# Retention and expert routing on one core: token keys of both heads in one place, scaled in place, and the state beside the values

## The chip, the cores and the metric

The kernel runs on 1 core of one Trainium2 chip. The metric is the device time of one execution in microseconds (us), lower is better. A core has TensorE (PE, with its weight loads shown apart as PEld), VectorE (DVE), ScalarE (ACT), GpSimd (POOL) and SyncE (SP), which here only issues DMAs and reads registers. The input loads and the weight loads are issued by SP, the token stores by ACT, and indirect gathers and scatters by POOL.

## What is computed

The reference has two halves. The first is retention, an attention with a decay in place of a softmax (8 batches, 8 heads, 576 positions, heads of 64):

```python
scores = scale * np.matmul(q, k.transpose(0, 1, 3, 2))
gamma = 1.0 - 2.0 ** (-5.0 - np.arange(H, dtype=np.float32))
Dmat = np.where(rel >= 0, gamma[:, None, None] ** rel[None, :, :], 0.0)   # rel = i - j
ret = scores * Dmat[None, :, :, :]
return np.matmul(ret, v).astype(np.float32)
```

Its output, laid out as 4608 tokens of 512 features, goes through the second half: tokens whose product with w_skip is not positive pass unchanged; each other token goes to the one of 8 experts with the greatest logit, which adds gate * (relu(x @ w1) @ w2), with 1024 hidden features, to it.

## The kernel before

**The retention stage.** The 4608 tokens are worked on in 36 groups of 128 tokens (NT = 36). A group is two chunks (c = 0, 1) of 64 positions, and nine chunks (NQ = 9) are one batch element. Heads go in four pairs (NPR = 4), one head of a pair on partitions 0 to 63, the other on 64 to 127; j counts the two. Retention is computed by chunks: the products inside a chunk (scores, line 469), and a running state of 64 by 64 for each head that carries what earlier chunks gave (state, line 520). For a group g the loop at line 697 does:

- keys(g + 1) on POOL (line 508): the keys by token, scaled by a table of decays, are written to a tile kn of two buffers. There are two operations of 64 partitions, since the keys of the two j lie in different places of the loaded tile.
- state(2g) and scores(2g + 2), in turn on PE: products of kn with the values are summed up in the PSUM tile ps_s, products of queries and keys go to psc. After each state comes a pair of ACT copies (line 542) of ps_s into the tile u of the next chunk, where the next products of values need it. The next state product adds to the same ps_s and so waits for the copies.
- values(2g - 2) and values(2g - 1) on PE (line 552): one product with 128 rows each takes 64 rows of values and 64 rows of state as its weights, and decayed scores and queries as the moving side. So the state must lie in the same place of u as the values, on the other half of the partitions.
- state(2g + 1) and scores(2g + 3), then decay(g + 1) on DVE (line 489), which multiplies scores by decays and writes them over u's keys by feature.
- stage_c (line 580): transposes on PE, an ACT copy, and the store of a finished group of tokens by ACT. In between come logits (every four groups), pieces of routing on PE and DVE (a list with due times, line 657), and, once the first expert is known, its weights (line 634): SP loads them, ACT and POOL split them into a high and a low part.

**The tile u and its loads.** u_g holds four places (s) of [2 chunks, 4 pairs, 64] float32, 2 KB in each partition. Partitions 0 to 63 hold in s = 0 to 3 queries, keys, values by token, keys by token; partitions 64 to 127 hold keys, queries, keys by token, values by token. It is loaded by two DMAs of 512 KB (load_half, line 433): places 0 and 1, the first half, and places 2 and 3, the second. There are five buffers (UBUFS) and loads are issued four groups ahead (UAHEAD). At the start of iteration g the first half of group g + 4 is asked for (line 700); its buffer is that of group g - 1, which is free after values(2g - 1). After the first block of products the second half of group g + 3 is asked for, with a dependence on that block (line 705). Both are on SP's queue, in which everything goes in order: a waiting DMA holds what is behind it, and so does the register load that reads the first expert's number (line 321).

The state copy for j writes u[halves[j], 3 - j], which holds the raw keys by token of that half. So it may only be written when keys has read them. At the start of a batch element the state is zero, and a memset on POOL (line 525) writes zeros there instead.

**Order.** PE's order is that of the program (manual_schedule, line 667). On the other engines a scheduler orders instructions by their dependences, except those put under keep_in_program_order.

**After the retention stage.** Expert 0's rows are gathered by POOL, whose index comes from DVE (close_first, line 282), and turned by early transposes (line 615). The experts then run from about 170 us to the end: products on PE in three float32r terms, weights loaded by SP, split by ACT and DVE.

Of the kernel before, what the change touches and what calls it, by code (L numbers as in the profile page):

```python
# [11 lines left out]
F32 = mybir.dt.float32  # L12
# [5 lines left out]
ALU = mybir.AluOpType  # L18
# [3 lines left out]
B, H, S, D = 8, 8, 576, 64  # L22
NTOK, DM, NE, DF = B * S, H * D, 8, 1024
P = 128
NT = NTOK // P
NQ = S // D
NPR = H // 2
# [15 lines left out]
UAHEAD = 4  # L43
UBUFS = UAHEAD + 1
# [12 lines left out]
def kernel(  # L57
# [9 lines left out]
    nc = tc.nc  # L67
# [15 lines left out]
    def keep_up(n):  # L83
        for _ in range(n):
            nc.tensor.matmul(ps_m, warm[:, :P], warm, start=True, stop=True)
# [329 lines left out]
    with ExitStack() as actx:  # L415
        ac = actx.enter_context(tc.tile_pool(name="ac", bufs=1))
        ap = actx.enter_context(tc.tile_pool(name="ap", bufs=2))
# [5 lines left out]
        tt_sb = ac.tile([P, 3, NQ + 1, NPR], F32, tag="tt", name="tt_sb")  # L423
# [5 lines left out]


        u_t = {}

        def load_half(g, s, after=None):
            if s == 0:
                u_t[g] = ap.tile([P, 4, 2, NPR, D], F32, tag="u", name=f"u_{g}", bufs=UBUFS)
            half = nc.sync.dma_start(
                u_t[g][:, s : s + 2].rearrange("p s c a i -> p (s c a i)"),
                qkv[g, s // 2],
            )
            if after is not None:  # L440
                tc.add_manual_dep(
                    half.ins,
                    after.name,
                    mybir.DependencyInfo(mybir.DependencyClass.Sync, mybir.DependencyReason.DATA),
                    reason="the second half begins behind a block of products",
                )

        def load_u(g):
            for s in (0, 2):
                load_half(g, s)  # L450

        def last_product():
            return next(i for i in reversed(nc.cur_bb.bb.instructions) if i.engine == mybir.EngineType.PE)
# [7 lines left out]
        nc.scalar.dma_start(wg_sb, wg)  # L461

        ps_s = pp.tile([P, NPR, D], F32, tag="s", name="ps_s")
        halves = [slice(0, D), slice(D, P)]
        kn_t, px_t = {}, {}

        psc_t = {}

# [38 lines left out]

        def keys(g):
            c0 = 2 * g % NQ
            kn_t[g] = ap.tile([P, 2, NPR, D], F32, tag="kn", name=f"kn_{g}")  # L510
            for j in range(2):
                h = halves[1 - j]
                nc.gpsimd.tensor_tensor(  # L513
                    kn_t[g][h],
                    u_t[g][h, 2 + j],
                    tt_sb[h, 0, c0 : c0 + 2, :].unsqueeze(3).broadcast_to([D, 2, NPR, D]),
                    ALU.mult,
                )

        def state(n):  # L520

            g, c = divmod(n, 2)
            if n % NQ == 0:
                for j in range(2):
                    nc.gpsimd.memset(u_t[g][halves[j], 3 - j, c], 0.0)
            if n % NQ == NQ - 1:
                return
            for a in range(NPR):
                for j in range(2):
                    h = halves[1 - j]  # L530
                    nc.tensor.matmul(  # L531
                        ps_s[halves[j], a, :],
                        kn_t[g][h, c, a, :],
                        u_t[g][h, 3 - j, c, a, :],
                        start=n % NQ == 0 and a == 0,
                        stop=a == NPR - 1,
                        skip_group_check=True,
                    )
                    yield
            g, c = divmod(n + 1, 2)  # L540
            for j in range(2):
                nc.scalar.copy(u_t[g][halves[j], 3 - j, c], ps_s[halves[j]])  # L542

        def in_turn(*products):

            products = list(products)
            while products:
                products = [p for p in products if next(p, p) is not p]
# [3 lines left out]
        def values(n):  # L552

            g, c = divmod(n, 2)
            if c == 0:
                px_t[g] = pp.tile([P, NPR, P], F32, tag="xt", name=f"pxt_{g}", bufs=2)
            pxt = px_t[g]
            for a in range(NPR):
                for j in range(2):
                    nc.tensor.matmul(  # L560
                        pxt[halves[j], a, c * D : (c + 1) * D],
                        u_t[g][:, 3 - j, c, a, :],
                        u_t[g][:, j, c, a, :],
                        start=c == 0 and a == 0,
                        stop=c == 1 and a == NPR - 1,
                        skip_group_check=True,
                    )
            if c == 1:
                b, o = divmod(g, NB)
                if o == 0:  # L570
                    xt_t[b] = ap.tile([P, NPR, NB * P], F32, tag="xt", name=f"xt_{b}")
                c0 = 2 * g % NQ
                nc.vector.tensor_tensor(
                    xt_t[b][:, :, o * P : (o + 1) * P].rearrange("p a (c i) -> p a c i", c=2),
                    pxt.rearrange("p a (c i) -> p a c i", c=2),
                    gt_sb[:, c0 : c0 + 2].rearrange("p c a i -> p a c i"),
                    ALU.mult,
                )
# [89 lines left out]
        mctx.__enter__()  # L668
        lt = None
        keys(0)  # L670
        def route(b):

# [23 lines left out]

        for g in range(NT):
            ahead = g + 1 < NT
            if g + UAHEAD < NT:
                load_half(g + UAHEAD, 0)  # L700
            if ahead:
                keys(g + 1)
            in_turn(state(2 * g), *([scores(2 * g + 2)] if ahead else []))
            if UAHEAD <= g + UAHEAD - 1 < NT and g:
                load_half(g + UAHEAD - 1, 2, last_product())
            if g < len(NKEEP):
                keep_up(NKEEP[g])
            if g:
                values(2 * g - 2)
                values(2 * g - 1)  # L710
            if g < 4:
                decays(g + 1)
            in_turn(state(2 * g + 1), *([scores(2 * g + 3)] if ahead else []))
            if ahead:
                decay(g + 1)
            if g >= 2:
                stage_c(g - 2)
            if lt is None:
                routing(0 if g == NT - 1 else 3 if g < starts[KCUT + 1] else 8)
            if lt is not None:  # L720
                logits_b(g // NB - 1 - (g % NB < 2), lt)
                route(g // NB - 1 - (g % NB < 2))
                lt = None
            if g > NB and g % NB == 1:
                lt = logits_a(g // NB - 1)
            weights()
        g = NT
# [25 lines left out]
    block = rt.tile([P, 1], F32, tag="block", name="block")  # L753
# [211 lines left out]
    with tc.For_i(0, nblock, 1):  # L965
# [31 lines left out]
        for f in range(NFC):  # L997
            if f + AHEAD < NFC:
                ws.append(split_w(load_w(0, f + AHEAD, [reg])))
            h = [mp.tile([P, CAP], F32R, tag=x, name=f"{x}_more_{f}", bufs=3) for x in ("hhi", "hlo")]  # L1000
# [64 lines left out]
```

## Time and profile before

| What | Value |
|---|---|
| Median of 3 runs | 438.65 us (432.28 to 443.81) |
| The profiled execution | 432.73 us |
| Its span, first to last instruction | 431.0 us |
| Mean granted TensorE clock | 0.983 |
| Instructions | 13306 |
| DMA traffic | 92.14 MB, 214 GB/s over the span |
| Loads of u | 72 of 512 KB, median 5.2 us from issue to landing |

The profile is of one execution. Busy times add up the records of an engine; matmuls overlap in their records, so a busy PE is not one at its peak. A row of a timeline is start, duration, engine, line, operation, output and inputs, shape, count, and in brackets the idle time before it with what ended it. A row of waits is engine, line, what it waited for, and us in total, number, longest. What ended a wait is inferred: of several it is the one that came last in this profile.

### The profile page before, as it was taken

To read this page: it belongs to the slowest core of one execution; us is meant where nothing else is said; L and a number is where in the kernel's file an instruction comes from. 1 tells how busy PE (TensorE), PEld (TensorE's weight loads), DVE (VectorE), ACT (ScalarE), POOL (GpSimd) and SP (SyncE) were. 2 spreads that over 40 slices of the span, in tenths; PEclk is the share of its full clock that TensorE was granted. 3 is DMA by queue.
4 is the path that set the end of the run, shared out by engine and by line. 5 is a ranking of instruction groups with operands and counts; after the bars stand their busy time and mean duration, and the time that the engine had idled before them with its cause. 6 is when DMAs were issued, how large, how long until landed. Compare 5 with 4: busy or idle time off the path is not lost. (4 is left out here: it accounts for less than half of the span.)

```text
span 431.0 us, 13306 instructions
## 1 busy us (share of the span) xinstructions
PE 391.7 (91%) x5482; PEld 351.7 (82%) x5484; DVE 276.3 (64%) x562; ACT 186.9 (43%) x360; POOL 160.4 (37%) x182
## 2 busy tenths in 40 slices
PE   7788988899988589999999999999999999999990
PEld 3576776677777467888999999999999999999980
DVE  2595598488589978848755554865654755656430
ACT  2255444454644457117444434444444445445210
POOL 4665564545555397150330042033141250400302
PEclk9899999999999989999999999999999999999996
DMA  8899989899986977255673455455465465642101
GB/s 311 301 326 314 344 304 314 313 327 307 365 310 232 338 284 240 98 149 207 203 230 117 146 172 193 147 173 185 150 212 172 162 207 173 200 144 77 52 0 52
DMA packets 29023, 92.14 MB, mean 214 GB/s; under 512 B 4119, under 2 KB 4247, under 8 KB 28960
## 3 DMA queue, kind: packets, MB, share of 16 engines
q1 hardware_dynamic: 19584, 71.31, 48.4%
q0 software_dynamic: 3616, 9.86, 6.7%
q10 hardware_dynamic: 5760, 10.09, 6.3%
q8 instruction: 44, 0.72, 0.7%
q14 instruction: 19, 0.16, 0.1%
HBM read 77.07 MB, written 14.55 MB: 213 GB/s over the span
## 5 line engine op out<-in xcount | busy, mean ns | idle before, releaser
L140 DVE TENSOR_TENSOR wlo_w<-w,whi_w 128x1024 fp32r<-128x1024 f32 x59 | 71.9, 1223 | 61.9 <-ACT whi_w L139 61.8
L513 POOL TENSOR_TENSOR kn<-u,tt_sb 64x512 f32<-64x512 f32 x72 | 77.3, 1073 | 67.2 <-PE psc L479 44.2
L843 POOL DMA_INDIRECT out<-rs,sidx x24 | 32.8, 1366 | 156.4 <-DVE rs L842 153.2
L139 ACT CAST whi_w<-w 128x1024 fp32r<-128x1024 f32 x59 | 61.6, 1051 | 61.5 <-PE py L387 59.4
L542 ACT COPY u<-ps_s 64x256 f32<-64x256 f32 x128 | 47.0, 367 | 65.6 <-issue 26.7
L387 PE MATMUL py<-hhi,whi_w 128*128 128x344 f32 (+6 forms) x224 | 70.6, 315 | 0.0
L387 PE MATMUL ph<-xhi,whi_w 128*128 128x344 f32 (+6 forms) x224 | 68.9, 308 | 0.0
L387 PE MATMUL py<-hhi,wlo_w 128*128 128x344 f32 (+6 forms) x224 | 67.8, 303 | 0.0
L387 PE MATMUL ph<-xhi,wlo_w 128*128 128x344 f32 (+6 forms) x224 | 67.8, 302 | 0.0
L387 PE MATMUL ph<-xlo,whi_w 128*128 128x344 f32 (+6 forms) x224 | 67.7, 302 | 0.0
L387 PE MATMUL py<-hlo,whi_w 128*128 128x344 f32 (+6 forms) x224 | 67.6, 302 | 0.0
L531 PE MATMUL ps_s<-u,kn 64*64 64x64 f32 x1024 | 48.8, 227 | 14.4 <-issue 6.4
L531 PEld LDWEIGHTS ps_s<-u,kn 64*64 64x64 f32 x1024 | 39.2, 135 | 26.8 <-issue 10.8
L495 DVE TENSOR_TENSOR u<-psc,dt_sb 64x512 f32<-64x512 f32 x72 | 49.6, 689 | 14.2 <-PE psc L479 8.9
L395 ACT ACTIVATE hhi<-ph 128x344 fp32r<-128x344 f32 (+8 forms) x61 | 26.0, 427 | 64.1 <-PE ph L387 57.0
L479 PE MATMUL psc<-u 64*64 64x64 f32 x1152 | 51.8, 227 | 1.9 <-DVE u L495 0.6
L560 PE MATMUL pxt<-u 128*64 128x64 f32 x1152 | 45.1, 231 | 3.2 <-issue 2.8
L479 PEld LDWEIGHTS psc<-u 64*64 64x64 f32 x1152 | 41.7, 136 | 5.3 <-issue 2.4
L560 PEld LDWEIGHTS pxt<-u 128*64 128x64 f32 x1152 | 39.1, 142 | 7.5 <-issue 4.6
L387 PEld LDWEIGHTS py<-hhi,whi_w 128*128 128x128 f32 x224 | 42.2, 188 | 0.9
L387 PEld LDWEIGHTS ph<-xhi,whi_w 128*128 128x128 f32 x224 | 42.3, 189 | 0.1
L387 PEld LDWEIGHTS ph<-xlo,whi_w 128*128 128x128 f32 x224 | 42.3, 189 | 0.1
(178 smaller groups left out, 645.0 us busy)
## 6 DMA issues: line engine op xcount, KB each, us to landing
u<-qkv SPq DMA_DIRECT2D x72, 512.0 KB, 5.2
w<-w SPq DMA_DIRECT2D x64, 512.0 KB, 3.7
out<-xn ACTq DMA_DIRECT2D x36, 256.0 KB, 5.4
out<-rs,sidx POOLq DMA_INDIRECT x24
xg<-out,gidx POOLq DMA_INDIRECT x21
dt_sb<-dtab ACTq DMA_DIRECT2D x1, 256.0 KB
gt_sb<-dtab ACTq DMA_DIRECT2D x1, 256.0 KB
wg_sb<-wg ACTq DMA_DIRECT2D x1, 64.0 KB, 8.8
```

The source lines that it names most:

```text
L139: nc.scalar.copy(hi, t)
L140: nc.vector.tensor_tensor(lo, t, hi.bitcast(F32), ALU.subtract)
L387: nc.tensor.matmul(ps, x, y, start=first and n == 0, stop=last and n == 3 * len(terms) - 1)
L395: nc.scalar.activation(hi, ph, AF.Relu)
L479: nc.tensor.matmul(psc_t[g][halves[j], c, a, :], u[halves[j], 1 - j, c, a, :], u[halves[j], j, c, a, :], start=c == 0 and a == 0, stop=c = ...
L495: nc.vector.tensor_tensor(u_t[g][h, j], psc[halves[j]], dt_sb[h, c0 : c0 + 2], ALU.mult)
L513: nc.gpsimd.tensor_tensor(kn_t[g][h], u_t[g][h, 2 + j], tt_sb[h, 0, c0 : c0 + 2, :].unsqueeze(3).broadcast_to([D, 2, NPR, D]), ALU.mult,)
L531: nc.tensor.matmul(ps_s[halves[j], a, :], kn_t[g][h, c, a, :], u_t[g][h, 3 - j, c, a, :], start=n % NQ == 0 and a == 0, stop=a == NPR - 1, ...
L542: nc.scalar.copy(u_t[g][halves[j], 3 - j, c], ps_s[halves[j]])
L560: nc.tensor.matmul(pxt[halves[j], a, c * D : (c + 1) * D], u_t[g][:, 3 - j, c, a, :], u_t[g][:, j, c, a, :], start=c == 0 and a == 0, stop ...
L843: put = nc.gpsimd.indirect_dma_start(out=out, out_offset=bass.IndirectOffsetOnAxis(ap=sidx[:n, k, e : e + 1], axis=0), in_=rs[:n], in_offs ...
```

## The change

u gets a fifth place. The second half is now loaded by two DMAs of 64 partitions and 256 KB each: partitions 0 to 63 (values, keys) into places 2 and 3, partitions 64 to 127 (keys, values) into places 3 and 4. So the keys by token of both halves lie in place 3 (KEYS), and one POOL operation of 128 partitions scales them in place; the tile kn is gone (4 KB in each partition with its two buffers, while five u tiles grow by 10 KB). The values of partitions 0 to 63 lie in place 2, those of 64 to 127 in place 4, and the other 64 partitions of these two places are free: the state is copied, and the zeros are written, there. The products take the same operands at their new places.

The loads of u are put under program order, and the first half of group g + 4 is asked for behind the values products of iteration g, after the second half of group g + 3; in iteration 0 it stays at the start.

```diff
@@ -429,21 +429,32 @@
 
 
         u_t = {}
+        halves = [slice(0, D), slice(D, P)]
+
+        V0, KEYS, V1 = 4, 3, 2
+        vals = (V0, V1)
 
         def load_half(g, s, after=None):
             if s == 0:
-                u_t[g] = ap.tile([P, 4, 2, NPR, D], F32, tag="u", name=f"u_{g}", bufs=UBUFS)
-            half = nc.sync.dma_start(
-                u_t[g][:, s : s + 2].rearrange("p s c a i -> p (s c a i)"),
-                qkv[g, s // 2],
-            )
-            if after is not None:
-                tc.add_manual_dep(
-                    half.ins,
-                    after.name,
-                    mybir.DependencyInfo(mybir.DependencyClass.Sync, mybir.DependencyReason.DATA),
-                    reason="the second half begins behind a block of products",
+                u_t[g] = ap.tile([P, 5, 2, NPR, D], F32, tag="u", name=f"u_{g}", bufs=UBUFS)
+                places = ((slice(0, P), 0),)
+            else:
+                places = tuple((halves[j], V1 + j) for j in range(2))
+            for rows, k in places:
+                half = tc.keep_in_program_order(
+                    nc.sync.dma_start(
+                        u_t[g][rows, k : k + 2].rearrange("p s c a i -> p (s c a i)"),
+                        qkv[g, s // 2, rows],
+                    )
                 )
+                if after is not None:
+                    tc.add_manual_dep(
+                        half.ins,
+                        after.name,
+                        mybir.DependencyInfo(mybir.DependencyClass.Sync, mybir.DependencyReason.DATA),
+                        reason="the second half begins behind a block of products",
+                    )
+            return half
 
         def load_u(g):
             for s in (0, 2):
@@ -461,8 +472,7 @@
         nc.scalar.dma_start(wg_sb, wg)
 
         ps_s = pp.tile([P, NPR, D], F32, tag="s", name="ps_s")
-        halves = [slice(0, D), slice(D, P)]
-        kn_t, px_t = {}, {}
+        px_t = {}
 
         psc_t = {}
 
@@ -507,22 +517,17 @@
 
         def keys(g):
             c0 = 2 * g % NQ
-            kn_t[g] = ap.tile([P, 2, NPR, D], F32, tag="kn", name=f"kn_{g}")
-            for j in range(2):
-                h = halves[1 - j]
-                nc.gpsimd.tensor_tensor(
-                    kn_t[g][h],
-                    u_t[g][h, 2 + j],
-                    tt_sb[h, 0, c0 : c0 + 2, :].unsqueeze(3).broadcast_to([D, 2, NPR, D]),
-                    ALU.mult,
-                )
+            k = u_t[g][:, KEYS]
+            ins = nc.gpsimd.tensor_tensor(
+                k, k, tt_sb[:, 0, c0 : c0 + 2, :].unsqueeze(3).broadcast_to([P, 2, NPR, D]), ALU.mult
+            )
 
         def state(n):
 
             g, c = divmod(n, 2)
             if n % NQ == 0:
                 for j in range(2):
-                    nc.gpsimd.memset(u_t[g][halves[j], 3 - j, c], 0.0)
+                    nc.gpsimd.memset(u_t[g][halves[j], vals[j], c], 0.0)
             if n % NQ == NQ - 1:
                 return
             for a in range(NPR):
@@ -530,8 +535,8 @@
                     h = halves[1 - j]
                     nc.tensor.matmul(
                         ps_s[halves[j], a, :],
-                        kn_t[g][h, c, a, :],
-                        u_t[g][h, 3 - j, c, a, :],
+                        u_t[g][h, KEYS, c, a, :],
+                        u_t[g][h, vals[j], c, a, :],
                         start=n % NQ == 0 and a == 0,
                         stop=a == NPR - 1,
                         skip_group_check=True,
@@ -539,7 +544,7 @@
                     yield
             g, c = divmod(n + 1, 2)
             for j in range(2):
-                nc.scalar.copy(u_t[g][halves[j], 3 - j, c], ps_s[halves[j]])
+                nc.scalar.copy(u_t[g][halves[j], vals[j], c], ps_s[halves[j]])
 
         def in_turn(*products):
 
@@ -559,7 +564,7 @@
                 for j in range(2):
                     nc.tensor.matmul(
                         pxt[halves[j], a, c * D : (c + 1) * D],
-                        u_t[g][:, 3 - j, c, a, :],
+                        u_t[g][:, vals[j], c, a, :],
                         u_t[g][:, j, c, a, :],
                         start=c == 0 and a == 0,
                         stop=c == 1 and a == NPR - 1,
@@ -696,8 +701,8 @@
 
         for g in range(NT):
             ahead = g + 1 < NT
-            if g + UAHEAD < NT:
-                load_half(g + UAHEAD, 0)
+            if g == 0:
+                load_half(UAHEAD, 0)
             if ahead:
                 keys(g + 1)
             in_turn(state(2 * g), *([scores(2 * g + 2)] if ahead else []))
@@ -708,6 +713,8 @@
             if g:
                 values(2 * g - 2)
                 values(2 * g - 1)
+                if g + UAHEAD < NT:
+                    load_half(g + UAHEAD, 0)
             if g < 4:
                 decays(g + 1)
             in_turn(state(2 * g + 1), *([scores(2 * g + 3)] if ahead else []))
```

## The prediction

> **What bounds the kernel now.** I read the page first, then the busy time by stage, the timelines of ACT, POOL, DVE, PE and SP, and last the DMA queues. These are the page's lines:
>
> ```profile
> span 431.0 us, 13306 instructions
> ...
> PE 391.7 (91%) x5482; PEld 351.7 (82%) x5484; DVE 276.3 (64%) x562; ACT 186.9 (43%) x360; POOL 160.4 (37%) x182
> ...
> q1 hardware_dynamic: 19584, 71.31, 48.4%
> q0 software_dynamic: 3616, 9.86, 6.7%
> q10 hardware_dynamic: 5760, 10.09, 6.3%
> ```
>
> The edit touches only the retention stage, which ends near 166 us; the first four of the next rows are stretches of it, the fifth is of the experts' stage. Columns: length, busy time of PE, PEld, DVE, ACT and POOL, PE clock, DMA share, GB/s.
>
> ```profile
> 10.00:15.00 5.00, 2.85 (x69) 1.81 (x69) 1.95 (x3) 1.95 (x6) 4.33 (x6) 0.90 1.02 410
> ...
> 21.60:137.00 115.40, 101.36 (x2861) 82.12 (x2860) 88.62 (x176) 57.51 (x139) 64.11 (x71) 1.00 0.91 320
> ...
> 139.00:147.00 8.00, 5.65 (x185) 5.05 (x180) 7.56 (x29) 3.12 (x7) 0.28 (x2) 1.00 0.86 290
> 147.00:166.00 19.00, 14.23 (x310) 10.93 (x310) 16.22 (x33) 10.34 (x22) 18.11 (x23) 0.91 0.80 287
> ...
> 200.00:240.00 40.00, 40.00 (x250) 38.68 (x249) 23.32 (x32) 17.70 (x27) 7.32 (x6) 1.00 0.60 199
> ```
>
> In the experts' stage PE has no gap, so what the retention stage gives up reaches the end. On POOL the keys of groups 4 and 32 begin at:
>
> ```profile
> 21.60 2.49 POOL L513 TENSOR_TENSOR kn<-u,tt_sb 64x512 f32<-64x512 f32 x2 [0.59 <-POOL kn L513]
> ...
> 136.93 2.18 POOL L513 TENSOR_TENSOR kn<-u,tt_sb 64x512 f32<-64x512 f32 x2 [2.16 <-PE psc L479]
> ```
>
> That is 115.3 us for 28 groups, 4.12 us each. What sets that period is seen on ACT in a stretch without routing work:
>
> ```profile
> 104.43 0.74 ACT L542 COPY u<-ps_s 64x256 f32<-64x256 f32 x2 [1.76 <-PE psc L479]
> ...
> 106.20 0.74 ACT L542 COPY u<-ps_s 64x256 f32<-64x256 f32 x2 [0.41 <-PE psc L479]
> ...
> 107.89 0.74 ACT L542 COPY u<-ps_s 64x256 f32<-64x256 f32 x2 [0.95 <-issue]
> ```
>
> Two pairs of state copies make a group, 1.7 to 1.8 us apart: a block of products, a pair of copies that frees ps_s, the next block. That chain gives 3.46 us (107.89 less 104.43); routing and logits add the rest up to 4.12. The keys are not on it, though the trace names POOL as a releaser:
>
> ```profile
> 41.38 2.15 POOL L513 TENSOR_TENSOR kn<-u,tt_sb 64x512 f32<-64x512 f32 x2 [1.30 <-PE psc L479]
> ...
> 41.63 0.74 ACT L542 COPY u<-ps_s 64x256 f32<-64x256 f32 x2 [1.26 <-issue]
> ...
> 42.48 0.29 PE L531 MATMUL ps_s<-u,kn 64*64 64x64 f32 x2 [0.66 <-POOL kn L513]
> ```
>
> PE starts at 42.48, just behind the copies (41.63 + 0.74 = 42.37); the first half of kn happens to end at 42.45. POOL's operation at 41.38 makes the keys of the group after, so it is not what PE needs. I therefore count no gain from keys in the steady stretch.
>
> There is one place where the keys do hold PE:
>
> ```profile
> SPq L321 <- DVE lead_id L261: 7.2, 1, 7.2
> ...
> 139.87 0.81 SPq L436 DMA_DIRECT2D u<-qkv  x2
> ...
> 146.83 2.15 POOL L513 TENSOR_TENSOR kn<-u,tt_sb 64x512 f32<-64x512 f32 x2 [7.72 <-PE ps_m L188]
> ...
> 149.01 0.74 ACT L542 COPY u<-ps_s 64x256 f32<-64x256 f32 x2 [3.98 <-POOL kn L513]
> ...
> 149.86 0.24 PE L531 MATMUL ps_s<-u,kn 64*64 64x64 f32 x1 [3.16 <-ACT u L542]
> ```
>
> SP waits 7.2 us for the first expert's number, and the loads behind it (the first half of group 34, then the second of 33) go out only at 139.87. Keys 33 begin at 146.83, when, as I read it, that second half has landed (PE, the named releaser, had used the old kn long before). They end at 148.98. The state copy at 149.01 overwrites raw keys, so it must wait for both key operations, and PE stands 3.16 us.
>
> **The change part by part.** Durations are those of the profiled execution: 432.73 us in all, 431.0 of it span.
>
> *Keys.* 72 operations become 36 over 128 partitions.
>
> ```profile
> L513 POOL TENSOR_TENSOR kn<-u,tt_sb x72: 1033/1042/1422, 6.7 to 158.0; 64x512 f32<-64x512 f32 x72
> ...
> L648 POOL TENSOR_TENSOR wlo_w<-w,whi_w x20: 717/726/744, 148.9 to 169.4; 128x256 fp32r<-128x256 f32 x20
> ```
>
> The price of one lies between 1.04 us (the same 512 elements in each partition) and 2 x 0.73 = 1.45 us (128 partitions, half the elements, doubled). I take 1.04: the row with the same operands and length. POOL loses 25 to 40 us of its 77 us of keys. In the steady stretch this is worth 0 by itself, since the copy chain sets the period. If the cover went, it would cost one key operation a group.
>
> *State copies and memsets.* As many and as long as before, to free places; the wait of copies and memsets on the raw keys goes. In the steady stretch 0 (above). At 149 us the copy no longer waits; PE can then begin its block when keys 33 and the first half of 34, whose scores share the block, are there. Second half 33 is now queued ahead of first half 34, so it lands about one transfer earlier and the first half takes its old landing, about 146.8. One 512 KB transfer costs 48.4% x 431 / 71.31 = 2.93 us for each MB, 1.53 us for 0.524 MB. Keys 33: 146.83 - 1.53 + 1.04 = 146.3. PE can start near 146.9 where it started at 149.86: **-3.0 us**. Late next is the gather of expert 0's rows: its index comes from DVE, which is busy 16.2 of 19 us here, and its landing already holds PE at the stage's end:
>
> ```profile
> 157.19 0.80 DVE L295 TENSOR_SCALAR gi<-ids 128x2 int32<-128x2 f32 x1
> ...
> 166.61 0.98 PE L620 MATMUL pt_early<-ident,xg 128*128 128x128 f32 x7 [0.70 <-DMA xg<-out,gi]
> ```
>
> If the gather does not move, almost nothing of the 3.0 passes: bounds 0 and -4.3 (3.0 and the 1.3 us that the granted clock of 0.91 costs in 14.2 us of PE work). I keep -3.0, because the shorter POOL time moves DVE too, as follows.
>
> *DVE behind POOL.* Small DVE operations stretch while a key operation runs:
>
> ```profile
> 123.86 2.17 POOL L513 TENSOR_TENSOR kn<-u,tt_sb 64x512 f32<-64x512 f32 x2 [2.31 <-PE psc L479]
> ...
> 124.09 0.84 DVE L170 TENSOR_TENSOR cum<-cum,cs 128x8 f32<-128x8 f32 x1
> ...
> 125.05 1.00 DVE L204 TENSOR_TENSOR gt<-gt,cp 128x8 f32<-128x8 f32 x1
> ...
> L228 DVE TENSOR_SCALAR r<-iota,trank x36: 304/315/1906, 65.8 to 178.8; 128x384 bf16<-128x384 f16 x36
> ...
> 131.94 2.95 DVE L228 TENSOR_SCALAR r<-iota,trank 128x384 bf16<-128x384 f16 x5
> ...
> 138.43 0.15 DVE L261 CAST lead_id<-top 128x1 int32<-128x1 f32 x1
> ```
>
> Each ends as one of the two key operations ends (124.93, 126.03). Five matches that take 5 x 0.315 = 1.6 us took 2.95, on the way to the expert's number at 138.43, for which SP waits. With about half of POOL's key time gone, the number comes some 1 us earlier, and so do the loads behind it. On PE I take **-1.0 us** over the four stretches of routing; bounds 0 (DVE idle elsewhere) and -5.
>
> *Loads.* The second half becomes two DMAs of 64 partitions and 256 KB: 36 more issues.
>
> ```profile
> L436 SPq DMA_DIRECT2D u<-qkv x72: 327/328/1287, 0.8 to 145.5; - x72
> ...
> SPq L436 <- PE psc L479: 69.7, 30, 4.7
> ...
> 138.40 1.15 PE L560 MATMUL pxt<-u 128*64 128x64 f32 x32
> ```
>
> 36 x 0.33 = 11.8 us of SP, inside the 69.7 us in which SP waits for PE anyway: 0; uncovered, 0.33 us a group. Before, the first half of g+4 waited for the values products of iteration g, and the second half of g+3 stood behind it. Now the second half goes when its block of products is done, the 1.15 us of values products sooner, and the first half, not needed until iteration g+3, gives way. That is 0 on the path in steady state.
>
> What 64 partitions cost the DMA engines, no row shows. Bounds: 0, as the price by the byte does not depend on size (2.93 us per MB on q1 and on q0, 2.69 on q10's 256 KB stores), and +1.53 us a group, if a half reaches half the engines' throughput. The DMA engines are busy 0.91 x 115.4 / 28 = 3.75 us of a group's 4.12, so up to +0.37 us a group is covered. The nearest row, q0's gathers and scatters, has blocks of fewer than 128 rows among it and is no dearer than whole loads; I take +0.2, which is covered: 0. [...] No row of this trace shows a transfer to one half.
>
> *Start.* POOL waits there for each second half (keys 1 at 10.39), with DMA full at 410 GB/s:
>
> ```profile
> 10.39 2.20 POOL L513 TENSOR_TENSOR kn<-u,tt_sb 64x512 f32<-64x512 f32 x2 [1.24 <-DMA u<-qkv]
> ...
> 12.62 0.74 ACT L542 COPY u<-ps_s 64x256 f32<-64x256 f32 x2 [1.91 <-POOL kn L513]
> ```
>
> One key operation is saved (-1.1); halves at the dear bound would land 3.1 us later by group 1. I take 0.
>
> **Sum:** 432.73 - 3.0 - 1.0 = 428.7. The profiled execution lies 5.9 us below the median of the runs, 438.65 (432.28 to 443.81); the same 4 us off that median gives 434.7. I forecast the middle, 431.7, and for this case alone 427 to 436.
>
> **The rivals.**
> *Slower: the DMA engines become the bound.* If the halves cost more than +0.37 us a group, the loads fall behind and the period is the DMA time. Halfway to the dear bound, +0.77, gives 4.52 us a group: 0.40 x 32 groups loaded after the start = 12.8, so 445.5. At the bound 5.28, +37, so 470. For it: the 0.91 share, and 1.02 in the start. Against it: the price by the byte is flat in three queues. [...]
> *Nothing moves.* The gather's index comes no earlier and PE waits at the early transposes for what it gained: 432.7. For it: DVE is busy 7.56 of 8 us from 139 to 147, and PE already waits there. Against it: DVE has POOL's stretches to lose.
> *A larger gain.* DVE gets all of its -5 and the tail its -4.3: 423.4. For it: the fast groups show 3.46 us, the mean is 4.12. Against it: PE's own logits and routing products fill part of that.
> *The wait merely moves:* if keys 33 still end last, since both of their transfers land late, the stall is about 1.2 us shorter instead of 3.0, 430.5; it lies inside the forecast.
>
> **How the numbers follow.** Forecast 0.45 (the moved wait in it), DMA bound 0.27, nothing 0.16, larger gain 0.12. A measurement here tells about 2%, some 9 us. Faster by more than that: the larger gain and 0.08 of the forecast, 0.20. Slower: nearly all of the DMA case, 0.25. Within: the other 0.55. The range 423 to 452 leaves out about 0.06 below and 0.11 above, where the halves cost more than about +1.0 us a group (432.73 + 32 x 0.6 = 452).
>
> **What would show it.** Right: 36 key operations near 1.04 us; no wait of ACT's state copies on POOL near 147 us and a PE wait there under 0.5 us; steady period 4.0 to 4.1 us a group with a DMA share still under 0.97; lead_id 1 us earlier; the stage over by 163 us. Wrong: a DMA share at 1.0 with fewer than 310 GB/s, POOL's keys waiting for DMA in group after group, scores products held by loads (the slower rival); or the early transposes waiting 3 us or more for the gather (nothing moves).

## The result, and the profile after

| | before | after |
|---|---|---|
| Median, us | 437.12 (432.28 to 443.81, 4 runs) | 458.95 (452.74 to 461.42, 4 runs) |
| Profiled execution, us | 432.73 | 456.71 |
| Mean granted TensorE clock | 0.983 | 0.953 |

The changed kernel is slower: ratio 1.050, 95% interval 1.040 to 1.060. The forecast was 431.7 us, with a range of 423 to 452. Ratios here and below leave out executions more than 1.5% above the fastest of the same kernel; the profiled ones of the first three experiments are among these and some 1% longer than the rest. These are the page's lines for it, the last two those of the issues of u's loads (number, size, us to landing):

```profile
span 455.0 us, 13348 instructions
...
PE 401.2 (88%) x5482; PEld 360.0 (79%) x5484; DVE 262.0 (58%) x562; ACT 187.5 (41%) x360; POOL 120.7 (27%) x146
...
q1 hardware_dynamic: 20160, 71.31, 54.1%
q0 software_dynamic: 3616, 9.86, 6.4%
q10 hardware_dynamic: 5760, 10.09, 6.3%
...
u<-qkv SPq DMA_DIRECT2D x36, 512.0 KB, 5.3
u<-qkv SPq DMA_DIRECT2D x72, 256.0 KB, 6.2
```

The same 71.31 MB on q1 hold the DMA engines for 54.1% of 455.0 us, 246.2 us; before it was 48.4% of 431.0, 208.6 us. The difference, 37.6 us, is 1.04 us for each of the 36 groups. On that queue only the number and shape of the second halves and the order of the loads changed; experiments below take number and order by themselves. The busy time by stage, in the same columns as before the change, shows what follows:

```profile
10.00:15.00 5.00, 2.94 (x36) 1.81 (x37) 0.69 (x1) 0.73 (x2) 2.85 (x5) 0.50 1.06 277
21.60:137.00 115.40, 94.13 (x2465) 76.55 (x2461) 66.92 (x140) 48.83 (x117) 29.92 (x35) 0.93 1.00 281
27.57:157.00 129.43, 105.93 (x2778) 86.07 (x2778) 76.53 (x176) 55.38 (x133) 33.95 (x40) 0.93 1.00 284
```

In the stretch from 21.60 to 137.00 the DMA share went from 0.91 to 1.00 and the rate from 320 to 281 GB/s: the DMA engines are full and move less. PE's granted clock fell from 1.00 to 0.93 there, but PE is idle for 21 of the 115 us. POOL's busy time fell from 64.11 to 29.92 us, and that bought nothing. The waits between 20 and 160 us and the one-line view of the keys say who stands for it:

```profile
POOL u L521 <- DMA u<-qkv: 60.0, 21, 4.2
```

```profile
L521 POOL TENSOR_TENSOR u<-u,tt_sb x36: 1033/1044/1557, 10.1 to 184.2; 128x512 f32<-128x512 f32 x36
```

Before, POOL's keys waited for a load in 4 places of 72. Now they wait for one 21 times in these 140 us. POOL's timeline places the loss; its rows are the keys of groups 0, 4, 32, 33 and 35, and the first expert's weights between them:

```profile
10.12 1.56 POOL L521 TENSOR_TENSOR u<-u,tt_sb 128x512 f32<-128x512 f32 x1 [7.03 <-DMA u<-qkv]
...
27.57 1.04 POOL L521 TENSOR_TENSOR u<-u,tt_sb 128x512 f32<-128x512 f32 x1 [3.48 <-DMA u<-qkv]
...
157.02 1.04 POOL L521 TENSOR_TENSOR u<-u,tt_sb 128x512 f32<-128x512 f32 x1 [2.71 <-DMA u<-qkv]
167.79 2.78 POOL L653 TENSOR_TENSOR wlo_w<-w,whi_w 128x256 fp32r<-128x256 f32 x4 [9.73 <-DMA u<-qkv]
170.53 1.05 POOL L521 TENSOR_TENSOR u<-u,tt_sb 128x512 f32<-128x512 f32 x1
...
184.20 1.03 POOL L521 TENSOR_TENSOR u<-u,tt_sb 128x512 f32<-128x512 f32 x1
```

Their counterparts before, beside the rows of groups 4 (21.60), 32 (136.93) and 33 (146.83) in the prediction:

```profile
6.73 1.04 POOL L513 TENSOR_TENSOR kn<-u,tt_sb 64x512 f32<-64x512 f32 x1 [3.64 <-DMA u<-qkv]
...
148.94 2.79 POOL L648 TENSOR_TENSOR wlo_w<-w,whi_w 128x256 fp32r<-128x256 f32 x4
...
156.92 1.04 POOL L513 TENSOR_TENSOR kn<-u,tt_sb 64x512 f32<-64x512 f32 x1
```

The early transposes, where the retention stage ends, on PE after the change and before it:

```profile
190.14 1.09 PE L625 MATMUL pt_early<-ident,xg 128*128 128x128 f32 x8
```

```profile
165.58 0.33 PE L620 MATMUL pt_early<-ident,xg 128*128 128x128 f32 x1
```

So the loss adds up like this:

| Stretch | before | after | difference |
|---|---|---|---|
| Start, to keys 4 | 21.60 | 27.57 | +6.0 |
| Keys 4 to keys 32, 28 groups | 115.3 (4.12 each) | 129.5 (4.62 each) | +14.1 |
| Keys 32 to keys 35 | 20.0 | 27.2 | +7.2 |
| Keys 35 to the early transposes | 8.7 | 5.9 | -2.7 |
| The rest of the span | 265.4 | 264.9 | -0.6 |

The sum is the 24.0 us between the spans. The experts' stage is unchanged. All of the loss is in the stage that loads u.

### The profile page after: what moved, and what is told of

It reads as the page before. It is cut to its first block, busy times and chain, and to the rows that moved or that the text cites. A ratio compares the mean times of both kernels' runs of the same rounds, so it can differ in the third digit from the quotient of the medians.

```text
span 455.0 us, 13348 instructions
## 1 busy us (share of the span) xinstructions
PE 401.2 (88%) x5482; PEld 360.0 (79%) x5484; DVE 262.0 (58%) x562; ACT 187.5 (41%) x360; POOL 120.7 (27%) x146
## 3 DMA queue, kind: packets, MB, share of 16 engines
q1 hardware_dynamic: 20160, 71.31, 54.1%
## 5 line engine op out<-in xcount | busy, mean ns | idle before, releaser
L536 PE MATMUL ps_s<-u 64*64 64x64 f32 x1024 | 53.4, 238 | 18.0 <-POOL u L521 9.7
L536 PEld LDWEIGHTS ps_s<-u 64*64 64x64 f32 x1024 | 42.4, 145 | 32.3 <-issue 15.7
L521 POOL TENSOR_TENSOR u<-u,tt_sb 128x512 f32<-128x512 f32 x36 | 39.1, 1087 | 98.3 <-DMA u<-qkv 71.6
L489 PE MATMUL psc<-u 64*64 64x64 f32 x1152 | 57.4, 239 | 3.9 <-issue 3.9
L565 PE MATMUL pxt<-u 128*64 128x64 f32 x1152 | 46.6, 234 | 12.5 <-issue 12.5
L578 DVE TENSOR_TENSOR xt<-pxt,gt_sb 128x512 f32<-128x512 f32 x36 | 24.9, 692 | 52.0 <-PE pxt L565 48.5
L565 PEld LDWEIGHTS pxt<-u 128*64 128x64 f32 x1152 | 40.3, 145 | 16.7 <-issue 13.9
L489 PEld LDWEIGHTS psc<-u 64*64 64x64 f32 x1152 | 45.9, 147 | 6.9 <-issue 4.4
```

What stands on the lines that cost most here:

```text
L489: nc.tensor.matmul(psc_t[g][halves[j], c, a, :], u[halves[j], 1 - j, c, a, :], u[halves[j], j, c, a, :], start=c == 0 and a == 0, stop=c = ...
L521: ins = nc.gpsimd.tensor_tensor(k, k, tt_sb[:, 0, c0 : c0 + 2, :].unsqueeze(3).broadcast_to([P, 2, NPR, D]), ALU.mult)
L536: nc.tensor.matmul(ps_s[halves[j], a, :], u_t[g][h, KEYS, c, a, :], u_t[g][h, vals[j], c, a, :], start=n % NQ == 0 and a == 0, stop=a == N ...
L565: nc.tensor.matmul(pxt[halves[j], a, c * D : (c + 1) * D], u_t[g][:, vals[j], c, a, :], u_t[g][:, j, c, a, :], start=c == 0 and a == 0, st ...
L578: nc.vector.tensor_tensor(xt_t[b][:, :, o * P : (o + 1) * P].rearrange("p a (c i) -> p a c i", c=2), pxt.rearrange("p a (c i) -> p a c i", ...
```

## Experiments

The theory after the result: a transfer that reaches partitions 0 to 63 alone, or 64 to 127 alone, holds the DMA engines much longer by the byte, and the loss is this and nothing else (the half theory). The rivals: the mere number of DMAs and of their issues (count), the pinned order of the loads (order), the keys scaled in place and the fifth place (layout), and later a limit on DMAs in flight.

**One part at a time.** The kernel before, with only its second half loaded as two DMAs of 64 partitions:

```diff
+            places = (slice(0, P),) if s == 0 else (slice(0, D), slice(D, P))
+            for rows in places:
-            half = nc.sync.dma_start(u_t[g][:, s : s + 2]..., qkv[g, s // 2])
+                half = nc.sync.dma_start(u_t[g][rows, s : s + 2]..., qkv[g, s // 2, rows])
...
```

> The kernel before, in which only the second half of each group's load is split into two DMAs of 64 partitions and 256 KB; places, keys, order as before. Half theory (a transfer to the partitions 0 to 63, or 64 to 127, alone costs the DMA engines nearly twice by the byte): the whole loss, 450 to 460 us, the SP queue's share of the engines' time up by 37 us as in the changed kernel, 4.5 to 4.7 us a group. Count theory (each more DMA costs a fixed time): the same. Order theory (the loads' new order on SP is what costs) and place theory (scaling in place, the fifth place): 433 to 440 us, 4.1 us a group.

Measured: 470.42 us, ratio 1.085 (1.075 to 1.095). This one part makes all of the loss, and more. From its page, and SP's waits between 20 and 140 us:

```profile
q1 hardware_dynamic: 20160, 71.31, 50.7%
...
L515 POOL TENSOR_TENSOR kn<-u,tt_sb 64x512 f32<-64x512 f32 x72 | 76.6, 1063 | 99.7 <-DMA u<-qkv 70.0
```

```profile
SPq L438 <- PE pxt L562: 72.2, 21, 9.3
```

q1 takes 239.9 us (50.7% of 473.2). That is 31 us more than before, where the half theory expected 37, yet the time rose by more than that. From keys 4 (26.89) to keys 32 (176.43) a group takes 5.34 us, above the expected 4.5 to 4.7, at a DMA share of 0.88. That is 4.70 us of the engines' time, close to the 4.62 of the change; the rest of the period is waiting. Here the second half of group g + 3 still stands in SP's queue behind the first half of g + 4, which waits 72.2 us for the values products; before the change it was 21.5 us in the same stretch. SP also waits 12.6 us there for three stores to land. The change itself lost less (1.050), and its order of loads, which takes the second half out from behind that wait, is by this reading what saves the rest. No run separates it from the keys scaled in place.

The second half as two DMAs by places instead, each of 256 KB over all 128 partitions:

```diff
+            parts_ = ((s, 2, 0, 2 * DM),) if s == 0 else ((s, 1, 0, DM), (s + 1, 1, DM, DM))
+            for k, m, c0, n in parts_:
+                half = nc.sync.dma_start(u_t[g][:, k : k + m]..., qkv[g, s // 2, :, c0 : c0 + n])
```

> The kernel before, in which the second half of each load is split into two DMAs of 256 KB by places, each over all 128 partitions (rows of 2 KB). As many DMAs as in the change, none to one half. Half theory: 433 to 441 us, the SP queue's time up by under 8 us. Count theory: 450 to 460 us. Order and place theories: 433 to 440 us.

Measured: 440.06 us, ratio 1.015 (1.006 to 1.024). The same number of DMAs, of the same size, costs 1.5% where it reaches all partitions, and q1's time is 213.2 us (48.1% of 443.2), 4.6 more than before. By the medians the count explains less than a third of the 5%, and by its interval less than half.

The kernel before with only the new order of the loads and program order for them:

```diff
-            if g + UAHEAD < NT:
-                load_half(g + UAHEAD, 0)
+            if g == 0:
+                load_half(UAHEAD, 0)
...
                 values(2 * g - 1)
+                if g + UAHEAD < NT:
+                    load_half(g + UAHEAD, 0)
```

> The kernel before with the change's order of loads alone: under program order, the second half of group g+3 ahead of the first half of g+4, which comes behind the values products. Half and count theories: no loss, 428 to 438 us; by my prediction's step for the tail the PE wait of 3.2 us near 150 us falls under 1 us, worth up to 3 us. Order theory: 445 us or more.

Measured: 435.83 us over 10 runs, ratio 1.004 (0.999 to 1.009). POOL, PE and DVE at the place where the prediction took 3.0 us:

```profile
147.49 2.16 POOL L515 TENSOR_TENSOR kn<-u,tt_sb 64x512 f32<-64x512 f32 x2 [6.32 <-DMA u<-qkv]
```

```profile
150.53 0.24 PE L533 MATMUL ps_s<-u,kn 64*64 64x64 f32 x1 [1.78 <-POOL kn L515]
...
157.03 0.28 PE L233 MATMUL ps_m<-mc,r 128*128 128x40 bf16 x3 [1.66 <-DVE r L228]
...
170.89 0.98 PE L622 MATMUL pt_early<-ident,xg 128*128 128x128 f32 x7 [1.82 <-DMA xg<-out,gi]
```

```profile
161.97 0.17 DVE L295 TENSOR_SCALAR gi<-ids 128x2 int32<-128x2 f32 x1
```

PE's wait fell from 3.16 to 1.78 us, not under 1 as expected, and PE then waits 1.66 us for the matches on DVE, and at the stage's end 1.82 us for the gather where it waited 0.70. The index gi comes no earlier than before (157.19). The order is worth nothing.

The change with its second half loaded whole:

```diff
-                places = tuple((halves[j], V1 + j) for j in range(2))
+                places = ((slice(0, P), V1),)
+                nc.gpsimd.memset(u_t[g][halves[1], V0], 0.0)
```

> The changed kernel, but the second half is one DMA of 128 partitions to places 2 and 3, and place 4 of partitions 64 to 127 is set to zero by POOL. It leaves out the values of half the heads (their output is zero), so tokens go to other experts and only the retention stage is to be compared. Half and count theories: 4.0 to 4.15 us a group, a DMA share of 0.93 or less, the keys of group 32 before 138 us. Order and place theories: 4.5 to 4.7 us a group as in the changed kernel, a DMA share of 0.97 to 1.

Measured: 474.81 us in all. This is no verdict, since other tokens go to other experts and the experts' stage grows. The retention stage can be compared. Keys 4 begin at 18.87 and keys 32 at 132.97:

```profile
18.87:132.97 114.10, 99.52 (x2858) 81.22 (x2856) 83.53 (x174) 57.34 (x138) 48.25 (x69) 1.00 0.93 323
```

That is 4.07 us a group (114.10 / 28) where the change has 4.62 and the kernel before 4.12. Everything of the change is in this run except the halves and the 36 more DMAs that they bring. Layout falls as a cause of the loss, and the start's loss is gone too (18.87 against 27.57).

**The transfers by themselves.** The next kernel only loads: twelve second halves in one form after another, with a DVE copy behind each form that ends it.

```python
for phase in phases:
    for i in range(12):
        phase(i)
    nc.vector.tensor_copy(sink, big[:, :, 0 : 2 * DM : DM // 2])
```

> Transfers alone: it leaves out the whole computation (the output is zeros). Ten phases of 12 second halves each, one phase after the other: whole (512 KB, 128 partitions); two DMAs to partitions 0 to 63 and 64 to 127 on SP; the same with the second on ACT's queue; two DMAs of 128 partitions by columns; four DMAs of 32 partitions, the halves in turn; four DMAs of halves by columns; partitions 32 to 95 alone; 0 to 63 alone; 64 to 127 alone; whole again. Port theory (what counts is which partitions a transfer reaches, 0 to 63 and 64 to 127 each half the way in): whole and by columns near 400 GB/s, halves near 210 on one queue, 32 to 95 alone near 400, 0 to 63 alone near 210; on two queues between the two. Partition-count theory (a DMA of 64 partitions is dear whichever they are): 32 to 95 alone near 210 too, four DMAs of 32 below 150.

The stretches between the copies, with busy DVE and POOL, clock, DMA share and GB/s: 256 KB columns over 128 partitions; partitions 32 to 95 alone; 0 to 63 alone; 64 to 127 alone; whole.

```profile
94.96:114.89 19.93, 0.00 (x0) 0.00 (x0) 1.00 0.89 316
175.57:187.94 12.37, 0.00 (x0) 0.00 (x0) 1.00 0.72 254
188.15:205.62 17.47, 0.01 (x2) 0.00 (x0) 1.00 0.87 180
205.83:223.65 17.82, 0.00 (x1) 0.00 (x0) 1.00 0.86 177
223.89:242.67 18.78, 0.00 (x0) 0.00 (x0) 1.00 0.85 335
```

The three middle rows carry the same 3.1 MB in the same twelve DMAs of 64 partitions. 32 to 95 take 12.37 us, 0 to 63 and 64 to 127 take 17.5 to 17.8, nearly as long as the whole load of twice the bytes. So at the same number of partitions and the same size the time depends on which partitions one transfer reaches. What tells these partitions apart, no run shows. The order of the forms is that of the port theory, the level is not: whole loads moved 335 and 32 to 95 moved 254 GB/s (at a DMA share of 0.72) where some 400 was expected, and 0 to 63 moved 180 where 210 was. The forms not shown took 27.03 us (two halves issued by SP and ACT, 233 GB/s), 27.31 (four DMAs of 32 partitions, 230 GB/s) and 32.65 (halves by columns); none comes near the whole load's 18.78. In this run the stores of the output still ran beside the first stretches, so the two halves behind one another were measured again without them:

> Transfers alone again, with the stores of the output behind everything (in the first such run they still ran beside the phase of two halves, so that its 34 us are not its own). It leaves out the whole computation. Phases of 12 second halves: whole; two DMAs to 0-63 and 64-127; the two forms in turn; 32-95 alone; 0-63 alone; two DMAs by columns over 128 partitions; whole; two halves again. Half theory: two halves 28 to 36 us where whole ones take 17 to 19, both times; in turn midway; 32-95 alone near 12, 0-63 alone near 17.5; by columns near 20. If two halves come out at 22 us or less, the price in the kernel (1.04 us a group) is not the halves' own but their meeting with other traffic.

Its stretches, in the same columns: whole, two halves, the two forms in turn, 32 to 95 alone, 0 to 63 alone; then whole and two halves once more.

```profile
0.72:19.50 18.78, 0.48 (x1) 0.00 (x0) 1.00 0.86 335
19.74:49.82 30.08, 0.00 (x1) 0.00 (x0) 1.00 0.94 209
50.03:74.29 24.26, 0.00 (x0) 0.00 (x0) 1.00 0.91 259
74.53:86.61 12.08, 0.01 (x1) 0.00 (x0) 1.00 0.75 260
86.82:104.45 17.63, 0.00 (x0) 0.00 (x0) 1.00 0.85 179
...
125.33:143.92 18.59, 0.00 (x0) 0.00 (x0) 1.00 0.87 338
144.16:173.68 29.52, 0.00 (x1) 0.00 (x0) 1.00 0.94 213
```

Two halves cost (30.08 - 18.78) / 12 = 0.94 us more for each 512 KB, and 0.91 the second time. The forms in turn take 24.26 us, near the mean of the two (24.4), so in this mixture their prices add. No other traffic is needed for the loss.

**Ways round it.** Four DMAs of 32 partitions, the two partition halves in turn:

```diff
-                places = tuple((halves[j], V1 + j) for j in range(2))
...
+                    (slice(j * D + i * quarter, j * D + (i + 1) * quarter), V1 + j) for i in range(2) for j in range(2)
```

> The changed kernel with each second half in four DMAs of 32 partitions, the two halves in turn. From the transfers alone (27.3 us for 12 where two DMAs took 34.0 and whole ones 18.8) the half theory, with port use evened out by turns, expects 0.7 us a group of the price in place of 1.27: 442 to 452 us. Count theory: 470 us or more.

Measured: 487.44 us, ratio 1.125 (1.113 to 1.137), far from what was expected. SP's waits between 40 and 140 us:

```profile
SPq L448 <- DMA out<-xn: 55.0, 14, 6.3
```

SP now waits 55 us for stores to land on which no load depends, and the DMA share falls to 0.75 from 21 to 137 us. q1's time rose by 22.7 us (47.5% of 486.9), 0.63 a group, near the 0.7 that the half theory gave it. The rest of the loss is not the engines' time: the loads are held back at their issue. That the program lets only so many DMAs be in flight at once is my reading; no view shows the number.

Less data in halves: keys with queries in one DMA of 768 KB, only the values in halves (2 x 128 KB); and the same with values in quarters.

```diff
-                places = ((slice(0, P), 0),)
+                places = ((slice(0, P), 0, 3),)
             else:
-                places = tuple((halves[j], V1 + j) for j in range(2))
+                places = tuple((halves[j], V1 + j, 1) for j in range(2))
...
```

> The changed kernel with its layout turned so that the keys by token come with queries and keys in one DMA of 768 KB over 128 partitions (places 0 to 2), and only the values go to one half each (two DMAs of 128 KB, rows of 2 KB). Half theory: the price is by the bytes that go to one half, so half of it remains: some +0.5 us of DMA time a group over the kernel before, 4.2 to 4.4 us a group, 437 to 447 us. Count theory (as many DMAs as in the change): 455 to 460 us. Place theory: 455 to 460 us.

> The two together: keys with queries and keys, the values in four DMAs of 32 partitions and 64 KB, the halves in turn. Half theory: a quarter of the price remains, 432 to 441 us; if the rest of the change is worth its 5 us (the retention stage of the run with whole loads), it is no slower than before. Count theory: 470 us or more.

Measured: 445.65 us, ratio 1.031 (1.020 to 1.041), and 481.8 us, ratio 1.116 (1.105 to 1.126). With half the bytes in halves the loss is some three fifths, and q1 takes 221.4 us (49.8% of 444.6), 12.8 more than before against 37.6 in the change. The total lies in the expected range, but the way there is not the expected one. The DMA share is only 0.88 at 4.54 us a group (4.2 to 4.4 were expected), which is 4.00 us of the engines' time, +0.25 where half the price was to be +0.5. So neither a price by the bytes in halves nor full engines explain this run, and what sets its period stays open. The quarters meet the same wait as above (38.5 us of SP for stores, a DMA share of 0.69).

If stores and loads share a limit, moving the stores' issue from ACT to POOL should free the loads. This was tried on the quarters and on the change itself:

```diff
-            nc.scalar.dma_start(out[g * P : (g + 1) * P, :], xn)
+            nc.gpsimd.dma_start(out[g * P : (g + 1) * P, :], xn)
```

> The run with second halves in four DMAs of 32 partitions (487 us), with the token stores issued by POOL instead of ACT. In that run SP waited 55 us for the landing of stores, though no load depends on a store: the program seems to allow only so many DMAs of SP and ACT in flight. In-flight theory: with the stores on another engine's queue SP's waits on landings fall to a third or less and the time to 450 to 470 us. Count theory (each DMA costs the engines): 480 us or more.

> The changed kernel with the token stores issued by POOL. Half theory alone: 452 to 461 us, DMA share of 0.97 or more as before. If the limit on DMAs in flight carries the loss: 445 us or less.

Measured: 532.73 us, ratio 1.229 (1.221 to 1.237), and 463.53 us, ratio 1.068 (1.060 to 1.075). The first is inconclusive: SP's waits for landings are gone, but POOL's stores wait for ACT and hold the keys behind them, as its waits between 40 and 140 us show.

```profile
POOL out L595 <- ACT xn L594: 61.7, 12, 6.4
...
PE ps_s L539 <- POOL u L524: 35.6, 15, 3.2
```

The second is clear on what it was for. SP has no waits for stores left, the time is slightly above the 452 to 461 us of the half theory and far from the 445 of the other, and the change is still at a full DMA share and nearly the same rate (281 GB/s before the stores were moved):

```profile
21.00:137.00 116.00, 94.66 (x2525) 76.53 (x2526) 70.50 (x141) 50.25 (x121) 43.62 (x59) 0.94 0.99 284
```

So a limit in flight does not carry the change's loss. That it carries the quarters' loss is not shown, since taking the wait away did not bring their time back.

**The change without halves.** Whole loads that bring values and keys of both halves into places 2 and 3; POOL copies the values of partitions 64 to 127 to place 4.

```diff
-                places = tuple((halves[j], V1 + j) for j in range(2))
+                places = ((slice(0, P), V1),)
...
+            nc.gpsimd.tensor_copy(u_t[g][halves[1], V0], u_t[g][halves[1], V1])
...
-    for s, (a, b) in enumerate(((hq, hk), (hk, hq), (rv, rk), (rk, rv))):
+    for s, (a, b) in enumerate(((hq, hk), (hk, hq), (rv, rv), (rk, rk))):
```

> The changed kernel with whole loads and a right result: values and keys by token of both halves arrive in places 2 and 3 in one DMA of 128 partitions, keys are scaled in place in one operation, and POOL copies the values of partitions 64 to 127 to place 4, beside which the state of 0 to 63 goes. Half theory: the loss is gone, 427 to 437 us, 4.0 to 4.15 us a group; by the retention stage of the run with whole loads (4.8 us shorter than before) it may be up to 5 us faster than before. Place and order theories: 450 us or more.

Measured: 431.82 us over 12 runs against 433.45 over 17 of the kernel before, ratio 0.993 (0.988 to 0.998): the same as the kernel before within 2%, and by the interval a little faster. From its busy time by stage, its page, and the timelines of POOL, DVE and PE:

```profile
21.00:137.00 116.00, 100.32 (x2861) 81.05 (x2854) 83.90 (x180) 57.43 (x139) 51.70 (x70) 1.00 0.90 316
```

```profile
L521 POOL TENSOR_TENSOR u<-u,tt_sb 128x512 f32<-128x512 f32 x36 | 37.8, 1049 | 75.2 <-DMA u<-qkv 66.6
```

```profile
19.11 1.04 POOL L521 TENSOR_TENSOR u<-u,tt_sb 128x512 f32<-128x512 f32 x1 [1.55 <-DMA u<-qkv]
...
134.38 1.04 POOL L521 TENSOR_TENSOR u<-u,tt_sb 128x512 f32<-128x512 f32 x1 [1.12 <-DMA u<-qkv]
```

```profile
130.97 2.63 DVE L228 TENSOR_SCALAR r<-iota,trank 128x384 bf16<-128x384 f16 x5
...
136.70 0.15 DVE L261 CAST lead_id<-top 128x1 int32<-128x1 f32 x1
...
156.09 0.17 DVE L295 TENSOR_SCALAR gi<-ids 128x2 int32<-128x2 f32 x1
```

```profile
164.93 1.09 PE L626 MATMUL pt_early<-ident,xg 128*128 128x128 f32 x8
```

The DMA share is back at 0.90 and the period at 4.12 us (keys 4 at 19.11, keys 32 at 134.38). One thing is to be read with care: POOL's keys still wait 66.6 us for DMA in the whole run here, and 71.6 in the change. A wait of an engine for data is a loss only where the engine is late for somebody. In these two runs the DMA share tells the two apart (0.90 here, 1.00 in the change).

## Why the prediction was wrong

**The step that failed** is the price of the halves: "The nearest row, q0's gathers and scatters, has blocks of fewer than 128 rows among it and is no dearer than whole loads; I take +0.2, which is covered: 0." Measured by themselves they cost +0.91 to +0.94 us a group. In the kernel the DMA engines' time per group went from 3.75 to 4.62 us, +0.87, and q1's time over the whole run rose by 1.04 a group. All lie between the half-way value (0.77) and the dear bound (1.53) of the prediction, above the cover of 0.37. The argument against the rival, that the price by the byte is flat in three queues, had no force: none of those queues was shown to carry transfers to one partition half alone, so their flatness said nothing about the reach of a transfer. The unknown price had bounds on both sides of the cover, and the value was taken from a row that differs in just what was in question.

**The rival was right in its mechanism.** For the DMA engines as the bound the prediction named the signs, a share of 1.0 with fewer than 310 GB/s and keys that wait for loads in group after group, and both came: 1.00 at 281 GB/s, and 60.0 us in 21 waits from 20 to 160 us. It had a chance of 0.27. By themselves, one half alone moved 177 to 180 GB/s where whole loads moved 335 to 338; in one run it was 179 of 335, 0.53, where the dear bound assumed half. Two halves moved 209 to 213, 17 to 19% more than the 179 of one half in the same run. The partitions 32 to 95 moved 254 to 260 GB/s with the same bytes as one half.

**The rival's sum was short in two places.** The measured +0.50 a group (4.62 less 4.12), put in place of its +0.40, gives 16 us over its 32 groups; the trace has 24. The start, for which it counted nothing and the forecast took 0 of a bound of 3.1 by group 1, lost 6.0, since DMA was the limit there already (from 10 to 15 us a share of 1.02 before and 1.06 after, at 410 and 277 GB/s). And the tail lost 7.2 between keys 32 and 35. The engines are full there too: the loads of the last groups share them with the first expert's weights, at a share of 0.99 from 157 to 168 us. But POOL's order changed as well. The split of these weights (167.79) now stands ahead of keys 33, where before it stood behind them (146.83, then 148.94). The DMA that its row names for its 9.73 us of idle time is not what it needs: ACT's first high part ends at 167.72, just before it starts. How the 7.2 us divide between the full engines and this order is not shown. SP's two waits for stores in this tail (6.5 and 5.5 us) are not needed for it: with the stores on POOL they are gone, and keys 32 to 35 take 26.8 us (160.65 to 187.43) where the change has 27.2.

**The tail, -3.0:** the wait was read rightly, what it is worth was not. The order alone took 1.4 us off it, and nothing of that reached the end. In the version with whole loads no state copy waits for POOL there, keys 33 begin 4.1 us earlier than before (142.74 against 146.83), and PE's longest wait for the copies is 1.15 us. Yet the early transposes begin only 0.65 us earlier (164.93 against 165.58): PE now waits 2.8 us for DVE's matches. That is the lower bound that the prediction named (0) and the rival "nothing moves" described, with the matches late next in place of the gather.

**DVE behind POOL, -1.0:** not borne out. In the change everything is later. In the version with whole loads the expert's number does come 1.7 us earlier (136.70 against 138.43), but keys 32 come 2.5 us earlier (134.38 against 136.93), by a lead that is there at keys 4 already (19.11 against 21.60). Counted from keys 32 the number comes 0.8 us later. The five matches on its way still take 2.63 us where they took 2.95. DVE's busy time from 21 to 137 us did fall, from 89.19 to 83.90, but no run shows a gain from it.

**Right:** the price of the keys (1.04 us for 128 partitions, median 1044 ns, not 1.45); that they are not on the path (POOL's busy time halved, and with whole loads the period is 4.07 to 4.12 us as before); that the order of the loads is worth nothing by itself, with whole loads. **Not quite right:** the 36 issues more, costed at 0. With all partitions reached, twice as many second-half DMAs cost 1.5%. It was not separated whether the issues, the shorter rows (2 KB instead of 4) or something else makes it.

The range missed the result by 7 us. It left a chance of 0.11 above, "where the halves cost more than about +1.0 us a group"; they cost about that, and the start and the tail, which had no term in that bound, did the rest.

## What to carry to other kernels

Before a load is split by partitions, ask which partitions each transfer reaches: in the transfers by themselves a split into 0 to 63 and 64 to 127 took 60% more time for the same bytes (30.08 against 18.78 us), and a column split over all 128 partitions 6 to 10% more (19.93 against 18.78 us, and 20.40 against 18.59). Here DMA was busy 0.91 of a group, and 0.87 us more a group made it the bound of the loop (a share of 1.00, 4.62 us a group where it was 4.12), whatever the layout saved on the engines; a copy of 64 partitions on POOL (0.61 us; POOL was busy 51.70 of 116 us with it) was the cheaper way to the same layout. When the nearest row differs from the new transfer in the very property that is in doubt, it sets no price: keep the bound, and give the rival its chance.

## What the runs showed of the hardware

- Two runs of twelve DMAs, each with the same 64 partitions' worth of bytes, differ by 46% in time by the starting partition alone (17.63 us from 0, 12.08 us from 32).
- On POOL an operation with 512 float32 a partition took 1.04 us over 128 partitions (median 1044 ns) as over 64 (1042 ns). Two such operations merged into one saved half of the time there (77.3 us of keys before, 39.1 after).
- With more DMAs, loads waited at their issue for stores that they do not depend on: with quarters SP stood 55.0 us for 14 landings of stores in 100 us. With halves it is less: 12.6 us for 3 landings in the kernel before with halves, none in the change between 20 and 140 us, and 12.0 us for 2 in its tail (162 to 192 us). That a limit on DMAs in flight is behind it is argued, not shown.
